# A reordered prologue, fewer pairs on VectorE, more zero matmuls and a split last block in an attention-and-convolution kernel

## The chip, the cores and the metric

The kernel runs on one core of one Trainium2 chip. The metric is the device time of one execution in microseconds (us). The span of a profiled execution, from its first to its last instruction, is about 2 us shorter than the device time (907.9 against 909.96 for the kernel before). Executions of one kernel differ in the clock granted to TensorE (0.993 to 1.000 in the runs of the kernel before), so the mean granted clock is given beside a time where it matters (1.000 is full speed).

The engines are TensorE (PE, its weight loads PEld), VectorE (DVE), ScalarE (ACT), GpSimd (POOL) and SyncE (SP). A "q" behind a name, such as SPq or ACTq, is that engine's issuing of transfers.

## The reference

Two results of the same input x (2048 rows of 640) are mixed by a gate. Cut to what matters:

```python
g = sigmoid((x * gate_w).sum(-1, keepdims=True))
# a: short convolution of k (4 taps) times v, long convolution by FFT, + kv*D, times q
# b: attention, 32 heads of 20, one shared key and value head
q = (x @ wq).reshape(B, S, 32, 20).transpose(0, 2, 1, 3)
k = x @ wk;  v = x @ wv
p = softmax(einsum("bhqd,bkd->bhqk", q, k) * 20 ** -0.5)
b = einsum("bhqk,bkd->bhqd", p, v)...reshape(B, S, 640) @ wo
return g * a + (1 - g) * b
```

The 32 heads x 2048 queries x 2048 keys need 134 million exponentials. They are computed in 2048 tiles of 128 x 512: 32 groups, each of 16 key blocks and 4 tiles.

## The kernel before

The kernel is written as a list of operations with costs and priorities. A list scheduler in the same file gives every engine its order and places the semaphores. A change of a priority, a constant or a list therefore reorders a large part of the program. ScalarE takes the tiles in units of three and two (ETA, ETB) from two sets of PSUM banks, while TensorE computes the scores of the next unit and multiplies the finished ones with the values (PV, into bank 6):

```python
def EXP(n):
    lo, w = 512 * base[n % 2], 512 * len(units[n])
    op("act", lambda e: e.activation(et(n)[:, 0:w], self.ps[:, lo:lo + w], ACT.Exp, scale=SCALE),
       [("ps", base[n % 2] + k) for k in range(len(units[n]))], [("ET", n % 4)], c_exp(w), name="exp", main=True,
       after=self.sins if n == 0 else ())
```

Some pairs of tiles are taken from ScalarE. DVE_J has one entry for each of the 32 groups, and each number in it is a key block of which VectorE exponentiates two tiles, by six instructions. The convolution, the projections and the output projection fill the gaps of TensorE.

Where a gap is left, the scheduler puts in a *zero matmul*: it adds zeros to bank 6, so it changes nothing. It is placed if, by the scheduler's own estimates, TensorE was busy for less than the share FILL of the last 2.4 us. It is not allowed between the last PV of a group and the first of the next (`can_fill`), as bank 6 is read then:

```python
if (self.filler is not None and self.main_started and self.can_fill and m is not None and gap > 0.1
        and self.busy_in(t, 2.4) < FILL):          # FILL = 0.55
    f = Op("pe", self.filler, c_mm(512), "c", "fill", 0.0)
...
self.can_fill = not op.last
...
sch.filler = lambda e: e.matmul(self.bank(6), self.T["zeros"][:, :], self.T["Tcos"][:, 0, 0:512], start=False,
                                stop=False)
```

The prologue has its own zero matmuls (filler0), under the same FILL. It brings x transposed: block 3 of 512 rows by a plain load and transposes on TensorE, blocks 0 to 2 by transposing transfers:

```python
self.dma(T["xn"][:, 12:16, :], x[:, 12:16, :], writes=[("xn", 3)], nbytes=655360, prio=-9)
for b in range(NB - 1):
    o = T["xT"][:, :, 512 * b:512 * b + 512]
    i = aps["A_q"][0][512 * b:512 * b + 512, :]
    xl = self.g.add("sp", lambda e, o=o, i=i: e.dma_start_transpose(o, i), (), [("xT", b)], 0.1, kind="d", ...)
```

After these come 20 matmuls of 41 columns for each block (k, v and gate), the query projection of block 0 (10 matmuls of 512 columns), a bound on the scores, a small transfer that puts it under the queries (qT<-cr), and the first scores.

The tail evicts the four last output blocks and stores them:

```python
for ci in range(4):
    ...
    self.dve(lambda e, ci=ci, i=i, osb=osb: e.scalar_tensor_tensor(
        ..., T["omgf"][:, i:i + 1], T["part"][:, ci, :]..., ALU.mult, ALU.add), ..., name="op2_ev")
    self.dma(self.aps["out"][0][128 * i:128 * i + 128, :], osb[:, :], reads=[("outsb", ci)],
             nbytes=163840, prio=p, name="st_out", eng="act" if ci % 2 else "sp")
```

## Time and profile before

The median of the first three runs is 908.3 us (907.63 to 909.58). The profiled run took 909.96 us, at a mean clock of 0.998.

| part of the span of 907.9 us | us | what limits it |
|---|---|---|
| to the start of the first exponential | 25.3 | transfers of x, projections, one small transfer |
| first to last exponential | 873.3 | ScalarE, busy for 870.4 |
| after the last exponential | 9.3 | evictions and stores |

The lines behind the table stand in the prediction. In them, the busy time of an engine in a stage is followed by its number of instructions, and the clock of a stage stands behind the engines.

### The profile page before, as it was taken

How to read it: one execution, taken by the hardware profiler on the slowest of the kernel's cores; microseconds unless marked ns; L12 is line 12 of the kernel's file. 1: busy time of each engine (PE TensorE's matmuls, PEld its weight loads, DVE VectorE, ACT ScalarE, POOL GpSimd, SP SyncE). 2: the span in 40 equal slices, each digit the busy share in tenths (PEclk: the TensorE clock that was granted, in tenths of full speed). 3: DMA queues.
4: the chain of work that ended last, by engine and by line, in shares of the span. 5: the costliest groups of instructions: out<-in, count | busy, mean ns of one | idle time of the engine just before them, and what ended most of it. 6: DMA issues, size and time to landing. Idle time of an engine off the chain costs nothing.

```text
span 907.9 us, 16333 instructions
## 1 busy us (share of the span) xinstructions
PE 853.1 (94%) x6950; PEld 350.7 (39%) x7013; DVE 631.9 (70%) x878; ACT 883.9 (97%) x791; POOL 380.2 (42%) x330
## 2 busy tenths in 40 slices
PE   6999999999999999999999999999999998998897
PEld 3344344443433344343333333343443332432233
DVE  5446743456766668876887778876678896787964
ACT  5999999999999999999999999999999999999995
POOL 2940056870426396154685213769125495000000
PEclk9999999999999999999999999999999999999999
DMA  7940300010000010000010200000000000301111
GB/s 162 200 134 9 65 19 20 7 37 18 20 19 14 9 41 19 19 19 13 13 37 19 56 20 13 19 8 18 20 19 14 18 4 25 93 13 35 64 35 52
DMA packets 58507, 32.69 MB, mean 36 GB/s; under 512 B 41154, under 2 KB 54466, under 8 KB 58434
## 3 DMA queue, kind: packets, MB, share of 16 engines
q1 hardware_dynamic: 56168, 31.05, 12.7%
q8 instruction: 55, 0.90, 0.4%
q10 hardware_dynamic: 2266, 0.59, 0.3%
q14 instruction: 18, 0.15, 0.1%
HBM read 18.01 MB, written 6.02 MB: 26 GB/s over the span
## 4 chain that ended last, share of the span: by engine, by line
ACT 64%; PE 29%; DMA 3%; SPq 2%; DVE 2%; issue 1%; DVEq 0%
ACT ETA L1055 39%; ACT ETB L1055 25%; PE ps L1023 8%; PE ps L1336 6%; PE ps L1097 6%; PE ps L1400 3%; PE ps L949 2%; PE ps L1270 1%; DMA kTr<-in_A_k_dram 1%; SPq L1253 1%; DMA rbc<-scr_d 1%; DMA xT<-in_A_q_dram 1%; PE ps L1434 1%; PE ps L1187 1%; SPq L722 1%
## 5 line engine op out<-in xcount | busy, mean ns | idle before, releaser
L1055 ACT ACTIVATE ETA<-ps 128x1536 bf16<-128x1536 f32 x384 | 571.3, 1488 | 3.5 <-PE ps L1097 2.2
L1055 ACT ACTIVATE ETB<-ps 128x1024 bf16<-128x1024 f32 x383 | 410.3, 1071 | 0.2 <-PE ps L1023 0.2
L1023 PE MATMUL ps<-qT,kT 21*128 21x512 bf16 x2048 | 302.5, 384 | 34.6 <-ACT ETA L1055 22.7
L1367 POOL TENSOR_TENSOR Pp<-X,K 128x512 f32<-128x512 bf16 x120 | 168.6, 1430 | 358.2 <-DVE K L1355 350.8
L1097 PE MATMUL ps<-ETA,vaug 128*32 128x512 bf16 x1150 | 196.1, 389 | 0.4 <-DVE acc L1151 0.3
L1097 PE MATMUL ps<-ETB,vaug 128*32 128x512 bf16 x766 | 188.1, 389 | 0.0
L1023 PEld LDWEIGHTS ps<-qT,kT 21*128 21x128 bf16 x2048 | 74.7, 91 | 223.2 <-ACT ETA L1055 122.9
L1085 DVE TENSOR_SCALAR dJ<-ps 128x512 uint32<-128x512 f32 x132 | 90.7, 687 | 43.8 <-PE ps L1023 43.4
L1093 DVE SCALAR_TENSOR_TENSOR ETd<-dJ,dE 128x1024 bf16<-128x1024 f32 x66 | 89.4, 1354 | 19.5 <-PE ps L1097 19.4
L1090 DVE SCALAR_TENSOR_TENSOR dE<-dJ,dE 128x1024 f32<-128x1024 uint16 x66 | 89.9, 1362 | 0.5
L1092 DVE SCALAR_TENSOR_TENSOR dJ<-dJ 128x1024 f32<-128x1024 uint16 x66 | 89.3, 1353 | 0.4
L1367 POOL TENSOR_TENSOR AB<-Pp 128x256 bf16<-128x256 f32 x80 | 77.4, 967 | 4.9
L1400 PE MATMUL ps<-AB,Tcos 128*128 128x256 bf16 x320 | 78.2, 275 | 0.8 <-DVE dJ L1085 0.6
L1097 PEld LDWEIGHTS ps<-ETA,vaug 128*32 128x32 bf16 x1150 | 47.7, 93 | 65.6 <-issue 63.0
L1400 PE MATMUL ps<-AB,Tsin 128*128 128x256 bf16 x280 | 69.3, 275 | 0.0
L1097 PEld LDWEIGHTS ps<-ETB,vaug 128*32 128x32 bf16 x766 | 45.3, 92 | 43.5 <-issue 42.9
L1367 POOL TENSOR_TENSOR Pp<-Pp 128x512 f32<-128x512 f32 x40 | 60.9, 1524 | 2.7
L1088 DVE TENSOR_SCALAR dE<-dJ 128x1024 uint32<-128x1024 uint32 x66 | 54.1, 820 | 0.5
L1336 PE MATMUL ps<-ssm_kT,Tsin 128*128 128x256 bf16 x320 | 53.7, 275 | 0.0
L1336 PE MATMUL ps<-kv,Tsin 128*128 128x256 bf16 x320 | 53.7, 275 | 0.0
L1336 PE MATMUL ps<-kv,Tcos 128*128 128x256 bf16 x320 | 52.0, 275 | 1.2 <-DVE kv L1410 0.5
L1336 PE MATMUL ps<-ssm_kT,Tcos 128*128 128x256 bf16 x320 | 51.8, 275 | 0.4 <-DVE dJ L1085 0.3
(135 smaller groups left out, 807.5 us busy)
## 6 DMA issues: line engine op xcount, KB each, us to landing
rbc<-scr_d SPq DMA_DIRECT2D x31, 256.0 KB
scr_o<-oTn SPq DMA_DIRECT2D x24, 128.0 KB, 1.8
xn<-in_A_q_dram SPq DMA_DIRECT2D x4, 640.0 KB
kv<-in_A_v_dram SPq DMA_DIRECT2D x4, 640.0 KB, 5.3
out_dram<-outsb SPq DMA_DIRECT2D x14, 160.0 KB, 1.8
oTp<-scr_o SPq DMA_DIRECT2D x12, 160.0 KB, 5.2
wog<-in_B_wo_dram SPq DMA_DIRECT2D x4, 200.0 KB
wo<-in_B_wo_dram SPq DMA_DIRECT2D x4, 200.0 KB, 3.3
```

The source lines that it names most:

```text
L949: o = self.mm(gr, lambda e, bk, gi=gi, dc=dc: e.matmul(self.bank(bk), T["wq_pad"][:, dc, 128 * gi:128 * gi + 128], T["xT"][:, dc, 512 * I: ...
L1023: return e.matmul(self.bank(bk), T["kT4"][32 * r:32 * r + 21, 128 * j:128 * j + 128], T[f"qT{G // 8 % 2}"][32 * r:32 * r + 21, G % 8, :], ...
L1055: op("act", lambda e: e.activation(et(n)[:, 0:w], self.ps[:, lo:lo + w], ACT.Exp, scale=SCALE), [("ps", base[n % 2] + k) for k in range(le ...
L1085: self.evac(gr, "dve", lambda e, bk, h=h: e.tensor_scalar(J[:, 512 * h:512 * h + 512], self.bank(bk), SCALE * LOG2E * 65536.0, EOFF * 6553 ...
L1088: V(lambda e: e.tensor_scalar(E[:, :], J[:, :], 7, 0x7F800000, ALU.logical_shift_left, ALU.bitwise_and), [kJ], ["dE"], c_fast(1024), **k)
L1090: V(lambda e: e.scalar_tensor_tensor(Ef, lo, ED, Ef, ALU.add, ALU.mult), [kJ, "dE"], ["dE"], c_ps(1024), **k)
L1092: V(lambda e: e.scalar_tensor_tensor(Jf, lo, EP, lo, ALU.add, ALU.mult), [kJ], [kJ], c_ps(1024), **k)
L1093: V(lambda e: e.scalar_tensor_tensor(T["ETd"][:, :], Jf, EQ, Ef, ALU.add, ALU.mult), [kJ, "dE"], ["ETd"], c_ps(1024), **k)
L1097: return op("pe", lambda e: e.matmul(self.bank(6)[32 * r:32 * r + 32, :], T["vaug"][:, j, :], src, start=(j == 0), stop=(j == NSC - 1), ti ...
L1336: o = self.mm(gr, lambda e, bk, lhs=lhs, rhs=rhs, comp=comp, n=n: e.matmul(self.bank(bk, 256, 256 * comp), lhs, rhs, start=(n == 0), stop= ...
L1367: f = lambda e: e.tensor_tensor(out, a, b, alu)
L1400: self.mm(gr, lambda e, bk, lhs=lhs, fc=fc, comp=comp, h=h: e.matmul(self.bank(bk, 256, 256 * h), lhs, AB[:, fc, :, comp, :], start=(fc == ...
```

## The change

It tries to make the start shorter and to relieve VectorE, and it has four parts.

1. **Prologue.** Blocks 2 and 3 of x come by plain loads and are transposed on TensorE; only blocks 0 and 1 come by transposing transfers. Priorities bring the projection, the squares and the evictions forward, and ScalarE's table load for Exp waits for the squares.
2. **Pairs.** VectorE gets 62 pairs in place of 66, in other groups.
3. **Zero matmuls.** FILL rises from 0.55 to 0.7: 281 of them in place of 149 in the long stage. The prologue has 18 in both.
4. **Tail.** Of the four last output blocks, block 1 is scaled by ScalarE and added to by GpSimd, beside VectorE.

```diff
-FILL = 0.55
+FILL = 0.7
-DVE_J = [(), (), (), (), (), (6,), (2, 9), (2, 9), (2, 9), (2, 9), (2, 9), (3, 7, 11, 13), ...]     # 66 pairs
+DVE_J = [(), (), (), (6,), (), (2,), (3, 7, 11, 13), (2, 6, 11), (2, 9), (2, 9), (2, 9), (2, 9), ...] # 62 pairs
+NX = 2
...
-        self.dma(T["xn"][:, 12:16, :], x[:, 12:16, :], writes=[("xn", 3)], nbytes=655360, prio=-9)
-        for b in range(NB - 1):
+        for b in range(NX, NB):
+            self.dma(T["xn"][:, 4 * b:4 * b + 4, :], x[:, 4 * b:4 * b + 4, :], writes=[("xn", b)], nbytes=655360,
+                     prio=-9)
+        for b in range(NX):
...
-            gr = self.group("kT", (1.16 if b == 0 else 4.0) + 0.1 * b, banks=ALLB if b == 0 else (7, 4, 5))
+            gr = self.group("kT", (1.95 if b == 0 else 4.0) + 0.1 * b, banks=ALLB if b == 0 else (7, 4, 5))
...
+        self.warm.deps.update(self.g.writer[("ksq", b)] for b in range(NB))
...
+            if ci == 1:
+                tmp = T["dE"][:, 0:D].bitcast(F32)
+                self.op("act", ... e.activation(tmp..., self.ps[...], ACT.Copy, scale=T["omgf"][:, i:i + 1]) ...)
+                self.pool(lambda e, ci=ci, osb=osb, tmp=tmp: e.tensor_tensor(osb[:, :], tmp, T["part"][:, ci, :], ALU.add), ...)
+            else:
               self.dve(... scalar_tensor_tensor as before ...)
```

Cut are the order of the gate_w load and the priorities of some evictions and squares of the prologue.

More of the change, by code (lines that the diff above doesn't have):

```diff
@@ L512 @@
 SIDE = (7, 5)
-DVE_J = [(), (), (), (), (), (6,), (2, 9), (2, 9), (2, 9), (2, 9), (2, 9), (3, 7, 11, 13), (2, 9), (6,), (3, 8, 13), (2, 9), (3, 9), (2, 9), (3, 7, 11, 13), (2, 7, 12), (2, 7), (3, 9), (2, 7), (1, 5, 9), (2, 7, 12), (3, 8, 13), (4, 11), (2, 6, 11), (2, 6, 11), (1, 4, 8, 12), (2, 9), (1, 5, 9)]
+DVE_J = [(), (), (), (6,), (), (2,), (3, 7, 11, 13), (2, 6, 11), (2, 9), (2, 9), (2, 9), (2, 9), (3, 8, 13), (2, 9), (2, 9), (2, 9), (2, 9), (2, 9), (4, 11), (2, 9), (3, 9), (2, 9), (2,), (3, 8, 13), (2, 9), (2, 7), (2, 9), (2, 7, 12), (3, 8, 13), (3, 9), (3, 8, 13), (2, 7, 12)]
 MAC_ALT = ()
+NX = 2
 SCALE = float(DH) ** -0.5
@@ L713, in loads @@
         self.dma(T["gw5"][:, :], aps["gate_w"].rearrange("(dc p) -> dc p", p=128), writes=["gw5"], nbytes=2000,
-                 eng="act", prio=-98.65)
+                 eng="act", prio=-98.9, lat=6.2)
         self.dma(T["wqst"][:, :, 0:160], wq[:, :, 0:160], writes=[("wqst", 0)], nbytes=204800, eng="act", prio=-98.6)
@@ L723, in loads @@
                             nbytes=655360, prio=-8 + b, lat=1.6)
-            xl.iss = 3.3
+            xl.iss = 4.8 if b == 0 else 3.3
         self.xl = [xl]
@@ L799, in tables @@
                             ["warm"], 1.5, prio=-1500.0, after=list(sins)))
+        self.warm = sins[-1]
         self.sins = sins
@@ L858, in xT @@
         T = self.T
-        b = NB - 1
-        for d0, nd in ((0, 2), (2, 2), (4, 1)):
-            gr = self.group("xT", 1.0, banks=(0, 1, 2, 3, 4, 5, 7))
+        for b, d0, nd in [(b, d0, nd) for b in range(NX, NB) for d0, nd in ((0, 2), (2, 2), (4, 1))]:
+            gr = self.group("xT", 1.0 + 0.01 * b, banks=(0, 1, 2, 3, 4, 5, 7))
             for dc in range(d0, d0 + nd):
@@ L870, in xT @@
                 "p (d t) -> p d t", d=nd), True)
-            self.evac(gr, "dve", None, (), [("xT", b)], 0.45, alts=al)
+            self.evac(gr, "dve", None, (), [("xT", b)], 0.45, alts=al, prio=-2000.0)
     def load_x(self):
@@ L875, in load_x @@
         x = self.aps["A_q"][0].rearrange("(i p) d -> p i d", p=128)
-        for b in range(NB - 1):
+        for b in range(NX):
             self.dma(T["xn"][:, 4 * b:4 * b + 4, :], x[:, 4 * b:4 * b + 4, :], writes=[("xn", b)], nbytes=655360,
@@ L908, in kproj @@
                         self.bank(bk, 41, 44 * ci), T["xT"][:, dc, 128 * tc:128 * tc + 128], T["wkv"][:, dc, 0:41],
-                        start=(dc == 0), stop=(dc == NDC - 1)), [("xT", b), "wk", "wv", "wg"], 0.05)
+                        start=(dc == 0), stop=(dc == NDC - 1)), [("xT", b), "wk", "wv", "wg"], 0.03)
             def view(bk, lo, n=20):
@@ L913, in kproj @@
             self.evac(gr, "act", lambda e, bk, b=b, view=view: e.activation(
-                T["ksq"][:, 4 * b:4 * b + 4, :], view(bk, 0), ACT.Square), (), [("ksq", b)], c_act(80))
+                T["ksq"][:, 4 * b:4 * b + 4, :], view(bk, 0), ACT.Square), (), [("ksq", b)], c_act(80), prio=-4500.0)
             self.evac(gr, "dve", lambda e, bk, b=b, view=view: e.tensor_copy(T["vaug"][:, 4 * b:4 * b + 4, 0:20],
@@ L945, in qproj @@
         par = I % 2
+        first = I == 0 and gs[0] == 0
         for gl, gi in enumerate(gs):
@@ L957, in qproj @@
             self.evac(gr, "dve", None, (), [("qT", par, gi)], 0.7,
-                      alts=self.copy_alts(qt[:, gi, :], lambda bk: self.bank(bk)))
+                      alts=self.copy_alts(qt[:, gi, :], lambda bk: self.bank(bk)), prio=-2500.0 if first else None)
             self.dve(lambda e, gi=gi, gl=gl: e.tensor_tensor(T[f"sq{gl}"][:, :], qt[:, gi, :], qt[:, gi, :],
                                                              ALU.mult),
-                     [("qT", par, gi)], [("sq", gl)], c_fast(512), prio=prio - 500, port=True, name="sq")
-        gr = self.group("q2", prio - 500, banks=banks)
+                     [("qT", par, gi)], [("sq", gl)], c_fast(512), prio=-5500.0 if first else prio - 500, port=True, name="sq")
+        gr = self.group("q2", -5500.0 if first else prio - 500, banks=banks)
         ind = T[f"IndG{ng}"]
@@ L969, in qproj @@
         ci, cr = T["ci"], T["cr"]
-        pr = -5000.0 if I == 0 and gs[0] == 0 else prio - 500
+        pr = -5000.0 if first else prio - 500
         self.evac(gr, "dve", lambda e, bk: e.tensor_scalar(
@@ L1232, in tail @@
                 mm(ci, half, 7)
-            self.dve(lambda e, ci=ci, i=i, osb=osb: e.scalar_tensor_tensor(
+            if ci == 1:
+                tmp = T["dE"][:, 0:D].bitcast(F32)
+                self.op("act", lambda e, ci=ci, i=i, tmp=tmp: e.activation(
+                    tmp.rearrange("p (h n) -> p h n", h=2),
+                    self.ps[:, 1024 * ci:1024 * ci + 1024].rearrange("p (h n) -> p h n", h=2)[:, :, 0:HD],
+                    ACT.Copy, scale=T["omgf"][:, i:i + 1]), ["omgf", ("ps", 2 * ci), ("ps", 2 * ci + 1)], ["dE"],
+                    c_act(D), prio=p, name="op2_ev")
+                self.pool(lambda e, ci=ci, osb=osb, tmp=tmp: e.tensor_tensor(osb[:, :], tmp, T["part"][:, ci, :], ALU.add),
+                          ["dE", ("part", ci)], [("outsb", ci)], c_pool(D), prio=p, port=True, name="op2_ev")
+            else:
+              self.dve(lambda e, ci=ci, i=i, osb=osb: e.scalar_tensor_tensor(
                 osb[:, :].rearrange("p (h n) -> p h n", h=2),
```

## The prediction

> **What bounds the kernel now.** I read the views in this order: the busy times by stage, the costliest groups, the timeline of the first 26 us and of the last 10 us, and the start times of all 767 exponentials from the timeline of ScalarE. The stages first (columns: busy us and instruction count of each engine, granted clock, DMA share, GB/s):
>
> ```profile
> core 0: us, PE busy (x) PEld busy (x) DVE busy (x) ACT busy (x) POOL busy (x), PEclk, DMA share, GB/s
> 0.00:25.30 25.30, 18.40 (x155) 8.72 (x157) 13.79 (x55) 13.55 (x23) 6.11 (x19) 0.93 0.66 146
> 25.30:898.60 873.30, 830.22 (x6764) 339.33 (x6824) 611.97 (x815) 870.36 (x768) 374.11 (x312) 1.00 0.12 32
> 898.60:907.90 9.30, 4.45 (x34) 2.68 (x32) 6.09 (x9) 0.01 (x1) 0.00 (x0) 0.95 0.26 91
> ```
>
> The run is a prologue of 25.3 us (until the first exponential starts), a stage of 873.3 us in which ScalarE is busy for 870.4, and a tail of 9.3 us after the last exponential. In the long stage ScalarE is the bound: VectorE has 261 us free, GpSimd 499. The work is nearly all in two rows of the costliest groups:
>
> ```profile
> L1055 ACT ACTIVATE ETA<-ps 128x1536 bf16<-128x1536 f32 x384 | 571.3, 1488 | 3.5 <-PE ps L1097 2.2
> L1055 ACT ACTIVATE ETB<-ps 128x1024 bf16<-128x1024 f32 x383 | 410.3, 1071 | 0.2 <-PE ps L1023 0.2
> ```
>
> The idle time before them is 3.7 us in all, so waits hardly matter. The two durations overlap: from start to start, by the timeline, the median is 1.33 us for a 1536-wide one and 0.91 for a 1024-wide one, 2.24 for a pair of five 512-column tiles. The mean pair is 872.65 us / 383 = 2.279. The 14 us above 383 x 2.24 are about 60 intervals lengthened by 0.13 to 0.9 us (eleven of them by over 0.3, together some 5 us) and jitter.
>
> The prologue is a chain of transfers, projections and one small transfer:
>
> ```profile
> 1.25 11.25 SPq L722 DMA_TRANSPOSE xT<-in_A_q_dram  x3
> ...
> 12.16 0.68 PE L907 MATMUL ps<-wkv,xT 128*128 128x41 bf16 x20 [1.55 <-DMA xT<-in_A_q_dram]
> ...
> 13.05 3.63 PE L949 MATMUL ps<-xT,wq_pad 128*128 128x512 bf16 x9 [0.22 <-issue]
> ...
> 22.74 0.73 SPq L565 DMA_DIRECT2D qT<-cr  x1
> ...
> 25.30 1.45 ACT L1055 ACTIVATE ETA<-ps 128x1536 bf16<-128x1536 f32 x1 [0.78 <-PE ps L1023]
> ```
>
> TensorE waits until 12.1 for the second transposed block of x although the query projection (L949) needs only the first; then those ten 512-column matmuls run slowly. Their starts in the timeline are 0.43 us apart instead of 0.22, and the stretches with the clock (PE busy, clock among the columns above) say why:
>
> ```profile
> 12.60:16.30 3.70, 3.48 (x18) 1.39 (x15) 2.13 (x10) 1.53 (x4) 0.00 (x0) 0.54 0.63 127
> 16.30:18.00 1.70, 1.70 (x23) 0.99 (x22) 1.28 (x6) 1.28 (x3) 0.00 (x0) 1.00 0.96 325
> ```
>
> Nine intervals x 0.21 = 1.9 us are lost to half clock. The tail ends with four VectorE evictions and a last store:
>
> ```profile
> 902.27 3.26 DVE L1233 SCALAR_TENSOR_TENSOR outsb<-ps,omgf,part 128x640 bf16<-128x640 f32 x4 [0.54 <-PE ps L1211]
> ...
> 905.56 0.36 ACTq L565 DMA_DIRECT2D out_dram<-outsb  x1
> ```
>
> [...]first matmuls 0.43 us apart until about 6 us, half clock again for about 3.6 us from 12.65, after 1.6 us idle. [...]Here transposes move 230 to 290 GB/s, the plain load of x some 350 (3.0 to 4.5 us). [...]
>
> **The change, part by part.**
>
> *Fewer pairs on VectorE.* The two lists hold 66 and 62 pairs. A pair is two 512-column tiles whose exponential VectorE computes in about 6.3 us (2 x 0.69 + 0.82 + 1.36 + 1.35 + 1.35). So 8 tiles move to ScalarE: 1916 become 1924. On the path: 8/5 x 2.279 = **+3.65 us**; nothing hides it, as ScalarE is full. VectorE gets 25 us back, which are worth nothing in themselves. They can only shorten intervals in which TensorE waited for a late VectorE pair; of the 5 us in long intervals I grant 0.5. The groups with four pairs go from three to one, and that one (group 6) comes early.
>
> *More zero matmuls.* The order of instructions shows 281 instead of 149 in the long stage, and 18 as before in the prologue. 132 x 0.216 = 28 us of TensorE time, in gaps. In the long stage the clock is already 1.00, so nothing can be won; intervals with zero matmuls in them are no longer than the others (mean excess 0.02 to 0.04 us against 0.045 in those without), so I count 0.
>
> *Prologue.* Blocks 2 and 3 of x now come by plain loads ahead of two transposing DMAs, and TensorE transposes both (40 matmuls, 6 evictions, 3 on each of two engines). The same bytes move, but the block that the projection needs comes third. One more plain load of 655 KB at 350 GB/s is 1.8 us: the first transposed block, which released TensorE at about 9.7, should land near 11.3. After it stand 60 matmuls of 41 columns (2.0 us at the measured 0.66 per 20) and the ten of the projection (2.2 us at full clock): they end at 15.5, against 16.7 before. Then, by the order: the last 20 of 41 columns (0.6), five key matmuls (1.1), four zero matmuls (0.9), the small ones (0.7): 18.8. Two VectorE steps of 0.67 and 0.47 with four of 0.14 between: 20.5. The small transfer took 1.86 from issue to landing: 22.4. Scores and start: 0.7. The first exponential would start at **23.1** at full clock. The table load and the squares no longer stand in the way (before, squares waited behind the table load until 20.0). At half clock the 60 small matmuls take about 1.6 us more and a part of the projection 0.5: 24.6 to 25.2. The idle time before the block lands is about 1.4 us (before 1.6)[...]: I give full clock 4 chances in 10. Mean: 0.4 x 23.1 + 0.6 x 24.9 = 24.2, so **-1.1 us**.
>
> *Tail.* VectorE does three evictions of 0.82 us instead of four and ends at about 904.7 instead of 905.5. The other block: ScalarE starts at about 902.55, takes 0.79 (a 512-column one with a pointer takes 0.69, plus 128 x 0.83 ns), and GpSimd adds. Its nearest row:
>
> ```profile
> L1367 POOL TENSOR_TENSOR Pp<-Pp 128x512 f32<-128x512 f32 x40 | 60.9, 1524 | 2.7
> ```
>
> For 640 columns that is an estimated 1.9 us: 905.3. And the order shows that ScalarE's queue issues this block's store ahead of the last block's, which so waits for GpSimd: issues at about 905.4 and 905.8, against 905.56 before. **0.0 to +0.3 us, say +0.1**: the 0.8 us saved are taken back.
>
> Sum: 3.65 - 0.5 - 1.1 + 0.1 = +2.1 us, 910.4. I lower it to **909.5**, since a new list of pairs may remove more of the long intervals than I can see.
>
> **Rivals.** First: the prologue gains much more, since a projection that is not held for the second block and stays at full clock saves 1.9 us at once; with 3 us gained and long intervals halved (-2.5) the time would be 906. For it: the idle 1.6 us and the half clock are plainly visible; against: the needed block now stands third in the queue. Second: the prologue gains nothing or loses, as [...]the transfers are slower than I think (kT-like transposes beside plain loads took 4.5 to 5.0 us to issue, against 3.0 alone): 912 to 913. Third: TensorE becomes the bound by its zero matmuls. It shows busy for 830 of 873 us, but that is modelled; 2.28 us per pair hold 5 scores and 5 value matmuls that overlap in groups. If each of the 132 delayed ScalarE by 0.03 us it would be 4 us; the intervals above speak against it.
>
> **Range and chances.** Prologue -3 to +0.5, stage +1 to +5.5, tail +-0.4, run to run +-1: 906 to 912.5. Two per cent are 18 us, which is out of reach both ways: within 2% 0.98.
>
> **What would show it.** The first exponential at 23 to 25.2 us (a later one: the block landed later); the clock between 11 and 17 us, 1.00 or about 0.5; the stage from first to last exponential 874 to 877.5 us, with the median pair still at 2.24; in the tail a GpSimd addition of 1.5 to 2 us and the last two stores issued after it by ScalarE. I would be wrong if the long stage grew by less than 2 us though 8 tiles came to it (then late pairs cost more than I saw), if the pair interval itself moved, or if the clock fell in the long stage.

## The result, and the profile after

The changed kernel took 909.79 us (median of 4 runs, 909.53 to 910.33); the kernel before took 908.87 in the median of its 4. The ratio is 1.0012, with a 95% interval from 0.9995 to 1.003. A ratio here is the mean time of one kernel's fast runs over the mean time of the other's fast runs of the same rounds, so it is not quite the ratio of the medians quoted. Executions over 1.5% slower than the fastest of the same kernel are left out of the means. The results are correct.

The stages of the changed kernel (columns as in the prediction):

```profile
0.00:22.45 22.45, 18.56 (x175) 9.70 (x175) 15.05 (x57) 14.72 (x25) 5.83 (x19) 1.00 0.69 164
22.45:898.76 876.31, 867.35 (x6958) 351.34 (x6958) 592.24 (x790) 874.36 (x772) 367.48 (x312) 1.00 0.12 32
898.76:908.50 9.74, 4.31 (x32) 2.74 (x32) 4.84 (x7) 0.80 (x2) 1.53 (x1) 0.99 0.19 68
```

The prologue is 2.85 us shorter than in the profile of before, the long stage 3.00 longer and the tail 0.45 longer: +0.6 us for the span. ScalarE is busy for 874.36 us of its stage where it was 870.36. The stage changed by the work given to ScalarE, and the rest of that time still holds next to no waits, as the costliest groups show (count, busy us, mean ns, idle before them):

```profile
L1061 ACT ACTIVATE ETA<-ps 128x1536 bf16<-128x1536 f32 x385 | 570.0, 1480 | 1.7 <-PE ps L1029 0.4
L1061 ACT ACTIVATE ETB<-ps 128x1024 bf16<-128x1024 f32 x385 | 407.7, 1059 | 0.3 <-PE ps L1029 0.3
...
L1499 PE MATMUL ps<-Tcos,zeros 128*128 128x512 bf16 x281 | 87.1, 384 | 0.0
```

The starts of the exponentials are 1.33 and 0.90 us apart in the median, as before. What the intervals hold above those medians is 16.5 us in all, against 17.0 before.

The timeline of the prologue after (start, length, engine, line, what was written from what, count, idle time before and what ended it), for the lines that the prediction shows of before:

```profile
1.78 9.27 SPq L726 DMA_TRANSPOSE xT<-in_A_q_dram  x2
...
11.23 1.17 PE L911 MATMUL ps<-wkv,xT 128*128 128x41 bf16 x40
...
13.11 2.32 PE L955 MATMUL ps<-xT,wq_pad 128*128 128x512 bf16 x10
...
19.95 0.73 SPq L567 DMA_DIRECT2D qT<-cr  x1
...
22.45 1.45 ACT L1061 ACTIVATE ETA<-ps 128x1536 bf16<-128x1536 f32 x1
```

And the stretch from 11 to 17 us, with the clock (1.00) behind the engines:

```profile
11.00:17.00 6.00, 5.81 (x98) 3.75 (x97) 5.36 (x21) 5.30 (x12) 0.63 (x1) 1.00 0.78 203
```

The ten matmuls of the projection now take 2.3 us in one row, where nine of them took 3.63. The clock stays at full speed after the transfer has landed, and the small transfer is issued 2.8 us earlier.

The timeline of the tail after:

```profile
902.35 2.47 DVE L1250 SCALAR_TENSOR_TENSOR outsb<-ps,omgf,part 128x640 bf16<-128x640 f32 x3 [0.61 <-PE ps L1217]
902.62 0.79 ACT L1242 ACTIVATE dE<-ps,omgf 128x640 f32<-128x640 f32 x1 [3.86 <-PE ps L1217]
...
903.49 1.53 POOL L1247 TENSOR_TENSOR outsb<-dE,part 128x640 bf16<-128x640 f32 x1 [150.67 <-ACT dE L1242]
...
905.05 0.86 ACTq L567 DMA_DIRECT2D out_dram<-outsb  x2
```

VectorE is done at 904.82 and GpSimd at 905.02. ScalarE's queue issues the stores of blocks 1 and 3 one behind the other after that, until 905.91. From there to the end of the span are 2.6 us; before, the last store was issued by 905.92 and 2.0 us followed.

### The profile page after: what moved, and what is told of

Same layout as the page of the kernel before. It is cut to its first block, busy times and chain, and to the rows that moved or that the text cites. A ratio compares the mean times of both kernels' runs of the same rounds, so it can differ in the third digit from the quotient of the medians.

```text
span 908.5 us, 16687 instructions
## 1 busy us (share of the span) xinstructions
PE 890.2 (98%) x7165; PEld 363.8 (40%) x7165; DVE 612.1 (67%) x854; ACT 889.9 (98%) x797; POOL 374.8 (41%) x331
## 4 chain that ended last, share of the span: by engine, by line
ACT 52%; PE 38%; issue 5%; DMA 1%; DVE 1%; POOL 0%; SPq 0%; POOLq 0%
ACT ETA L1061 32%; ACT ETB L1061 20%; PE ps L1029 11%; PE ps L1353 8%; PE ps L1103 8%; PE ps L1417 5%; PE ps L1499 2%; PE ps L955 2%; PE ps L1287 1%; DMA kTr<-in_A_k_dram 1%; PE ps L1451 1%; PE ps L1503 1%; POOL Pp L1384 0%; PE ps L971 0%; SPq L1270 0%
## 5 line engine op out<-in xcount | busy, mean ns | idle before, releaser
L1384 POOL TENSOR_TENSOR Pp<-X,K 128x512 f32<-128x512 bf16 x120 | 166.5, 1413 | 346.4 <-DVE K L1372 345.5
L1091 DVE TENSOR_SCALAR dJ<-ps 128x512 uint32<-128x512 f32 x124 | 85.1, 686 | 36.3 <-PE ps L1029 35.3
L1099 DVE SCALAR_TENSOR_TENSOR ETd<-dJ,dE 128x1024 bf16<-128x1024 f32 x62 | 84.1, 1356 | 22.1 <-PE ps L1103 21.6
L1096 DVE SCALAR_TENSOR_TENSOR dE<-dJ,dE 128x1024 f32<-128x1024 uint16 x62 | 86.9, 1401 | 0.7
L1499 PE MATMUL ps<-Tcos,zeros 128*128 128x512 bf16 x281 | 87.1, 384 | 0.0
L1098 DVE SCALAR_TENSOR_TENSOR dJ<-dJ 128x1024 f32<-128x1024 uint16 x62 | 83.2, 1342 | 0.2
```

The lines of the kernel that those rows point to most:

```text
L1091: self.evac(gr, "dve", lambda e, bk, h=h: e.tensor_scalar(J[:, 512 * h:512 * h + 512], self.bank(bk), SCALE * LOG2E * 65536.0, EOFF * 6553 ...
L1096: V(lambda e: e.scalar_tensor_tensor(Ef, lo, ED, Ef, ALU.add, ALU.mult), [kJ, "dE"], ["dE"], c_ps(1024), **k)
L1098: V(lambda e: e.scalar_tensor_tensor(Jf, lo, EP, lo, ALU.add, ALU.mult), [kJ], [kJ], c_ps(1024), **k)
L1099: V(lambda e: e.scalar_tensor_tensor(T["ETd"][:, :], Jf, EQ, Ef, ALU.add, ALU.mult), [kJ, "dE"], ["ETd"], c_ps(1024), **k)
L1384: f = lambda e: e.tensor_tensor(out, a, b, alu)
```

## The experiments

My theory was the prediction's sum: a prologue that gains, eight more tiles on ScalarE that cost some 3 us, a tail that takes its gain back by the order of stores in one queue, zero matmuls that do nothing. Its rivals were that the zero matmuls delay ScalarE, that they carry the clock, and that the shorter prologue came from the clock alone. All runs gave correct results. All that follow are on one chip except w1_hole_filled, whose runs of the kernel before are its own. Each had five rounds. Ratios are against the kernel before. By the line of 2% all are rated "same" except x1_prologue (unclear) and y3_nozero (slower), so what follows on differences of a few us rests on the intervals and on the traces.

### The prologue alone: x1_prologue

The changed kernel with the other three parts undone. Its scheduler leaves out two of the prologue's 18 zero matmuls, so even the prologue is not quite the same:

```diff
-FILL = 0.7
+FILL = 0.55
-DVE_J = [... 62 pairs ...]
+DVE_J = [... the 66 pairs of before ...]
-            if ci == 1:
+            if ci == 99:
```

> The changed kernel with 66 pairs, old zero-matmul rule and old tail: of the four parts only the prologue stays. My theory (the parts add up: prologue -2.9 us as the first exponential came at 22.45 instead of 25.30 in the two profiles, pairs +3.0, tail +0.4, zero matmuls 0) expects 2 to 3.2 us less than before, about 906.0. Its own scheduler puts the key projection before the query projection here and leaves out two zero matmuls, so the first exponential may come at 22.5 to 23.5. Rival (the prologue's gain is an accident of one profile[...]): within 1 us of before.

Measured: 930.11 us (919.05 to 934.25), a ratio of 1.0207 (1.0158 to 1.0256), rated unclear. The first exponential starts at 22.74, near the 22.45 of the full change, but the long stage took 886.67. TensorE in stretches, with the clock (columns: length, PE busy and count, clock, DMA share, GB/s):

```profile
575.00:580.00 5.00, 3.94 (x36) 1.00 0.00 0
580.00:585.00 5.00, 4.79 (x25) 0.64 0.03 3
585.00:610.00 25.00, 25.00 (x128) 0.50 0.05 16
610.00:615.00 5.00, 5.00 (x28) 0.50 0.01 3
615.00:620.00 5.00, 4.92 (x40) 0.95 0.00 0
```

For some 34 us TensorE ran at half clock in the middle of the long stage, and the profile shows it busy for all of that time (25.00 of 25.00 us, by modelled ends). The timeline shows what came just before:

```profile
580.21 0.39 PE L1029 MATMUL ps<-qT,kT 21*128 21x512 bf16 x3 [0.95 <-ACT ETA L1061]
```

It had stood idle for 0.95 us, and 1.2 us after the end of that hole, at 581.4, its matmuls became slow. The clocks of the six runs were 0.957 to 0.983, and the times follow them: 919.05 us at 0.983, 932.1 at 0.961 (a slow run of 934.25 at 0.957 is left aside). So this run does not isolate the prologue: a change in the program's start reordered the long stage, and its clock fell. It raised the question of what the zero matmuls are for.

### The list of pairs alone: x2_62pairs

The kernel before with the 62 pairs in place of the 66, nothing else (151 zero matmuls in the long stage).

```diff
-DVE_J = [... 66 pairs ...]
+DVE_J = [... 62 pairs ...]
```

> The kernel before with only the new list of 62 pairs. Theory: 8 more tiles on ScalarE, stage from first to last exponential longer by 3.0 us (as between the two profiles) to 3.65, so 3 to 3.7 us slower, about 912. Rival (fewer pairs pay by fewer long intervals): less than 2 us slower.

Measured: 913.96 us (911.87 to 918.65), ratio 1.0063 (1.0033 to 1.0093), clocks 0.987 to 0.998. In its profile too the clock fell, for some 7 us:

```profile
480.00:488.60 8.60, 7.59 (x60) 1.00 0.23 46
488.60:495.00 6.40, 6.40 (x29) 0.50 0.00 0
```

Its two runs at a clock of 0.998 took 911.87 and 911.96. The kernel before took 907.88 to 909.47 in its four runs at that clock, 908.6 in the mean. The list alone costs about 3.3 us where the clock is alike, near the predicted 3.15, and further time where it falls.

### The tail alone: x3_tail

The kernel before with the split block alone.

```diff
+            if ci == 1:
+                (ScalarE scales into dE, GpSimd adds, as in the change)
```

> The kernel before with only the split tail. Theory: the eviction saved on VectorE (0.8 us) is taken back because ScalarE's queue issues two stores one after the other behind the GpSimd addition: 0 to +0.5 us. Rival (the longer tail of the changed kernel's profile, 9.74 against 9.29, was chance and the split pays): 0.4 to 0.8 us faster.

Measured: 908.11 us (907.82 to 910.14), ratio 0.9996 (0.9974 to 1.0017). The time can't tell 0.1 us from 0.4. The tail of the profile is 9.64 us; in the three profiles with the old tail it is 9.24 to 9.30. The engines behave as in the changed kernel (ScalarE 0.79 us, GpSimd 1.53, both late stores on ScalarE's queue).

The profile serves a second purpose. It has the old prologue, with the idle time before the second block, and the clock nevertheless held:

```profile
12.44 0.68 PE L907 MATMUL ps<-wkv,xT 128*128 128x41 bf16 x20 [1.73 <-DMA xT<-in_A_q_dram]
12.96 1.24 PE L949 MATMUL ps<-xT,wq_pad 128*128 128x512 bf16 x5
```

Its first exponential starts at 24.00. Half clock in the old prologue thus varies from profile to profile: of its four, two have it (25.30 and 25.40, with a mean clock of 0.93 up to there) and two do not (24.00 and 24.07, with 1.00).

### The change with as few zero matmuls as before: x4_fill55

```diff
-FILL = 0.7
+FILL = 0.55      # long stage: 149 zero matmuls; the prologue keeps 0.7
```

> The changed kernel with the old number of zero matmuls in the long stage (149 instead of 281), all else as changed, the prologue too. Theory: the clock is 1.00 in the stage either way, so within 0.5 us of the changed kernel (909.8). Rival A (the added zero matmuls delay scores): 1 to 3 us faster. Rival B (they keep the clock or shorten the long intervals): over 1 us slower, with a granted clock under 1.00 somewhere in the stage.

Measured: 911.31 us (910.32 to 913.39), ratio 1.0028 (1.0006 to 1.005). Four runs had a clock of 1.000 (mean 910.9) and two of 0.995 and 0.996 (913.39, 912.79).

```profile
23.25:900.37 877.12, 844.61 (x6826) 341.63 (x6826) 595.46 (x790) 874.30 (x772) 372.24 (x312) 1.00 0.12 32
```

TensorE is busy for 23 us less than with 281, yet the stage is 0.8 us longer, not shorter. So the added zero matmuls did not delay ScalarE (stages of 876.31 and 877.12 us).

### The changed kernel again: y1_after

No edit.

> The changed kernel itself, on the chip of the next three and with more rounds, as their reference. Expected: 909.5 to 910.5, within 0.3% of before, granted clock 0.998 to 1.000 in every run (it was so in its four runs).

Measured: 909.98 us (908.95 to 912.34), ratio 1.0017 (0.9992 to 1.0042). First exponential 22.12, stage 876.15, tail 9.63: the three stages repeat within 0.4 us. Against it, x4_fill55 is slower by 1.2 us in the mean of all runs and by 1.35 in those at a clock of 1.000. It was run at another time. So the sign is not firm.

### The old pairs with many zero matmuls: y2_66f65

With the 66 pairs of before and FILL = 0.7 the scheduler finds no end, as its last matmuls find no room, so 0.65 was used (220 zero matmuls).

```diff
-FILL = 0.7
+FILL = 0.65      # the prologue keeps 0.7
-DVE_J = [... 62 pairs ...]
+DVE_J = [... the 66 pairs of before ...]
```

> The changed kernel with the old list of 66 pairs, and zero matmuls between the two kernels' numbers (220 in the long stage; with 281 its scheduler finds no end). The prologue's instructions are those of the changed kernel. The first set left one question: the prologue with 66 pairs and 143 zero matmuls ran 919 to 934 us, as the clock stood at 0.50 from 581 to 615 us. Theory (TensorE was too idle there and zero matmuls are what prevents it): clock 0.998 or more, and 3 to 3.7 us faster than the changed kernel, about 906.5. Rival (66 pairs with the new prologue make a hole that zero matmuls do not fill, or pairs late on VectorE stall the stage): a clock under 0.99 and over 912 us.

Measured: 913.33 us (912.83 to 931.03, the longest a slow run at a clock of 0.970), ratio of fast runs 1.005 (1.0027 to 1.0073). The stage took 881.87 us in the profile, with half clock from about 552 to 569 us, after two holes of 0.60 and 0.42 us within 1.4 us. 220 zero matmuls did not keep the clock here.

### No zero matmuls in the long stage: y3_nozero

```diff
-FILL = 0.7
+FILL = 0.0       # the prologue keeps 0.7
```

> The changed kernel without any zero matmul in the long stage (0 instead of 281); the prologue's stay. My prediction counted them as worth 0. Theory as it stands after the first set (they keep TensorE busy enough that the clock does not fall): stretches of clock 0.50 in the stage, mean clock 0.95 to 0.99 and 5 to 25 us slower than the changed kernel, differing from run to run by several us. Rival (as predicted, worth nothing): within 1 us of it.

Measured: 1005.71 us (1002.78 to 1016.73), ratio 1.108 (1.1035 to 1.1125), clocks 0.834 to 0.855. The bulk of the long stage, and ScalarE's largest group:

```profile
24.00:960.00 936.00, 890.02 (x6495) 337.96 (x6493) 573.83 (x772) 854.79 (x744) 363.86 (x311) 0.85 0.11 29
```

```profile
L1062 ACT ACTIVATE ETA<-ps 128x1536 bf16<-128x1536 f32 x385 | 566.5, 1471 | 77.7 <-PE ps L1030 46.7 <-PE ps L1104 29.4
```

ScalarE's own instructions are as long as before, but it waits 77.7 us for TensorE before its wide ones, where it waited 1.7. TensorE has less to do, takes more time for it (890 us busy), and becomes the bound. Up to 900 us it stood idle for 0.5 us or more some 40 times (28 us in all; 4 times and 3.1 us in the changed kernel), and its score matmuls (L1030) took 436 ns in the mean, against 384 in the changed kernel. The zero matmuls are what keeps this kernel at full clock: 0.85 for the stage without them, 1.00 with 281.

### The split block's store on the other queue: y4_storesp

```diff
-nbytes=163840, prio=p, name="st_out", eng="act" if ci % 2 else "sp")
+nbytes=163840, prio=p, name="st_out", eng="act" if ci == 3 else "sp")
```

> The changed kernel with the split block's store issued by SyncE (after its other two) instead of by ScalarE, so that the last block's store no longer waits for the GpSimd addition. Theory (the queue order takes the saving back): the last block's store is issued at about 904.9 instead of 905.5 and the other at 905.1, and the run is 0.2 to 0.6 us faster than the changed kernel. Rival (the end is set by the addition and the landing of its store alone): within 0.1 us.

Measured: 909.12 us (908.51 to 911.33, and one slow run of 929.42 at a clock of 0.973), ratio of fast runs 1.0005 (0.9979 to 1.0031). The tail is 8.93 us:

```profile
902.28 2.12 SPq L567 DMA_DIRECT2D out_dram<-outsb  x3
...
903.86 0.37 ACTq L567 DMA_DIRECT2D out_dram<-outsb  x1
```

ScalarE issues block 3 at once, and SyncE issues block 1 after GpSimd. GpSimd's addition ends at 904.04, and the last issue at 904.40 in place of 905.91, while this run's last exponential ended 1.0 us earlier than the changed kernel's; 2.3 us follow. With the same two engines doing the same work, the tail is 0.7 us shorter than in y1_after, so what took the gain back was the order of two stores in one queue (three later profiles with this order have tails of 8.86 to 8.93). In the time it is 1.1 us in the mean of fast runs, inside their scatter.

### The old prologue with the rest of the change: z1_oldpro

The kernel before with the new pairs, FILL of 0.7 in the long stage (282 zero matmuls; 0.55 in the prologue) and the new tail.

```diff
-FILL = 0.55
+FILL = 0.7       # the prologue keeps 0.55
-DVE_J = [... 66 pairs ...]
+DVE_J = [... 62 pairs ...]
+            if ci == 1: (as in the change)
```

> The changed kernel with the old prologue: 62 pairs, the new tail and 282 zero matmuls in the long stage, so that the clock holds in the stage, unlike in the first set's attempt to show the prologue alone. Theory: the first exponential at 24.0 us, or at 25.3 where the clock halves at 12.6 us (seen in one of three profiles of the old prologue), against 21.7 to 23.25 in six profiles of the new: 1.7 to 2.5 us slower than the changed kernel, about 912. Rival (the new prologue takes part of its gain back in the first stretch of the stage): under 1 us slower.

Measured: 915.76 us (912.42 to 924.32), ratio 1.0091 (1.0054 to 1.0127), clocks 0.987 to 1.000. Two falls of the clock stand in the profile, one in the prologue and one in the stage, the latter behind an idle stretch:

```profile
12.00:16.00 4.00, 3.59 (x28) 0.57 0.72 143
...
745.60:755.00 9.40, 9.40 (x57) 0.64 0.51 121
```

```profile
745.29 0.39 PE L1024 MATMUL ps<-qT,kT 21*128 21x512 bf16 x3 [0.95 <-ACT ETA L1056]
```

Its two runs at a clock of 1.000 took 912.42 and 912.52; those of y1_after took 908.95 to 910.25, 909.5 in the mean. That is 2.9 us for the new prologue, if nothing else differed. The stage was ordered anew, so this is a rough estimate; the start times of the first exponential measure the prologue better. The rival's mechanism, a gain that is partly taken back in the first stretch of the stage, is in the traces; "Why the prediction was right or wrong" has the numbers.

### Other lists of pairs: z2_64pairs and z3_66pairs

Both start from y4_storesp. The first gives two groups one more pair each (64) and raises FILL to 0.8 (300 zero matmuls). The second adds two more pairs (66 again, but not those of before) at 0.7 (251 zero matmuls).

```diff
 z2: FILL = 0.8 (prologue 0.7); DVE_J[5] = (2, 9); DVE_J[22] = (2, 9)
 z3: FILL = 0.7;                DVE_J[5] = (2, 9); DVE_J[22] = (2, 9); DVE_J[9] = (2, 7, 12); DVE_J[14] = (2, 7, 12)
```

> Attempt at a version that beats both: the changed kernel with the split block's store on SyncE, two pairs more on VectorE (64: one more in groups 5 and 22, which had one each), and 300 zero matmuls. Theory (a pair is worth 0.9 us as long as the clock holds): 1.6 us faster than the same with 62 pairs (909.1), about 907.5, clock 0.998 or more. Rival (any move of the pairs opens holes in TensorE's work): clock under 0.997 and over 910.

> The same with four pairs more (66, in groups 5, 9, 14 and 22) and 251 zero matmuls, as its scheduler finds no end with more. Theory: 3.3 us faster than with 62 pairs, about 905.8, if the clock holds at 251 zero matmuls. Rival (66 pairs leave too little room for zero matmuls, as in the runs with the old list of 66): a stretch of clock 0.50, over 910.

Measured for z2_64pairs: 912.68 us (911.56 to 923.5), ratio 1.0067 (1.0033 to 1.0101), clocks 0.983 to 1.000. The most zero matmuls so far, and the clock fell again, after a hole of 0.95 us:

```profile
770.35 0.39 PE L1030 MATMUL ps<-qT,kT 21*128 21x512 bf16 x3 [0.95 <-ACT ETA L1062]
```

Measured for z3_66pairs: 907.17 us (906.59 to 907.85), ratio 0.9983 (0.997 to 0.9996), a clock of 1.000 in all five runs. It has the shortest time of all versions, ahead of both kernels by a little. Its long stage:

```profile
23.00:896.79 873.79, 864.84 (x6928) 350.07 (x6928) 614.13 (x814) 870.70 (x769) 378.97 (x312) 1.00 0.12 31
```

With 66 pairs the stage is back to within 0.5 us of before, with the short prologue (23.0 us) and the short tail (8.9) beside it. It holds the clock with fewer zero matmuls than two versions that lost it. So their number does not decide it.

### The holes at the groups' ends closed: w1_hole_filled

The holes of 0.95 us stand where a zero matmul is not allowed, at the end of a group. Here z2_64pairs may put one there into a side bank (7 or 5) that is free.

```diff
+            if (self.filler is not None and self.main_started and not self.can_fill and m is not None and gap > 0.1
+                    and ... and self.busy_in(t, 2.4) < FILL):
+                for b in (7, 5):
+                    if bank b is free: zero matmul into it, start=True, stop=True
```

> The 64-pair version (z2, 912.7 us, clock 0.983 to 1.000) with one rule more: zero matmuls may also stand where a head group's sums are being read out, into a free bank, which the old rule forbids. The order of instructions shows 308 instead of 300 zero matmuls, and the two score units that stood side by side at 770 us, with 0.95 us of idle TensorE between them, no longer do. In all five profiles with a fallen clock in the stage the fall came 0 to 2 us after such a hole (two score units with nothing between, or a wait of that length). Theory (the hole, not the number of zero matmuls, lets the clock fall): no hole of 0.8 us late in the stage, clock 0.998 or more in most runs, about 908. Rival (the clock falls for another reason): clock 0.997 or less and 911 to 913 again.

Measured on another chip: 909.02 us (908.3 to 909.94), ratio 0.999 (0.9977 to 1.0004), clocks 0.999 or 1.000 in all five runs, and 1.00 for the whole stage in the profile. The place that corresponds to the hole, in its timeline:

```profile
767.88 0.39 PE L1038 MATMUL ps<-qT,kT 21*128 21x512 bf16 x2
768.20 1.04 PE L1510 MATMUL ps<-Tcos,zeros 128*128 128x512 bf16 x4
769.17 0.39 PE L1038 MATMUL ps<-qT,kT 21*128 21x512 bf16 x3
```

Four zero matmuls fill it, with only eight more in all than z2_64pairs. Idle times of 0.5 us or more sum to 1.4 us in this stage. The ratio went from 1.0067 to 0.999. The stage took 876.01 us, though by its tiles (four fewer than in the changed kernel's 876.31 us, at 0.45 us each from the median intervals) I estimate some 1.5 us less; where that went is open. That it ran on another chip is a rival; the kernel before was no steadier there, with clocks of 0.996 to 1.000.

### What the runs say together on the clock

| run | zero matmuls in the stage | fall of the clock in the profiled stage | clocks of the fast runs |
|---|---|---|---|
| x1_prologue | 143 | yes | 0.961 to 0.983 |
| x2_62pairs | 151 | yes | 0.987 to 0.998 |
| y2_66f65 | 220 | yes | 0.989 to 0.994 |
| z1_oldpro | 282 | yes | 0.987 to 1.000 |
| z2_64pairs | 300 | yes | 0.983 to 1.000 |
| x4_fill55 | 149 | no | 0.995 to 1.000 |
| y1_after | 281 | no | 0.998 to 1.000 |
| z3_66pairs | 251 | no | 1.000 |
| w1_hole_filled | 308 | no | 0.999 to 1.000 |

In the five profiles with one, the first slow matmul comes 0.3 to 1.7 us after a hole: one of 0.95 us in three of them, several of 0.4 to 0.6 us in x2_62pairs and y2_66f65. The half clock then lasted 3.4 us in z2_64pairs, some 7 us in x2_62pairs and z1_oldpro, 17 us in y2_66f65 and some 34 us in x1_prologue. The theories of x1_prologue, y2_66f65, z1_oldpro and z2_64pairs, which added up parts at full clock, missed by this. A hole is not enough, though. The changed kernel has the same one, without a fall behind it:

```profile
741.35 0.39 PE L1029 MATMUL ps<-qT,kT 21*128 21x512 bf16 x3 [0.95 <-ACT ETA L1061]
```

That the holes matter is shown by y3_nozero (28 us of holes of 0.5 us or more, a clock of 0.85) and, less firmly, by w1_hole_filled (1.4 us, a clock of 1.00). Why the clock fell after one hole of 0.95 us and not after another was not shown: no run moves a hole and leaves the rest as it was.

## Why the prediction was right or wrong

The predicted 909.5 us stands beside 909.79 measured (909.98 when repeated), and "within 2%" held. The terms of the sum:

- **Fewer pairs (+3.65 and -0.5, so +3.15): right in size, partly by luck.** The stage grew by 3.00 us between the two profiles; the three profiles of the changed stage (876.31, 876.15, 876.06) stand 3.3 above the two of the old one (873.31, 872.37) in the mean. The median intervals did not move, as predicted; at them, eight tiles are 3.6 us. The excess above the medians fell by 0.5, as granted, but as the sum of two larger parts. The intervals longer by over 0.3 us went from 11 with 5.0 us together to 5 with 2.0, while the many small excesses grew by 2.6. Some of that growth belongs to the prologue: in the first 15 us of the stage the excess is 0.1 to 0.3 us in the four profiles of the old prologue and 0.95 to 1.3 in nine of the new (y3_nozero has 3.5). One part of it is seen: in the changed kernel TensorE waits 0.94 us at 33.9 for a transfer of the convolution (kTr), and the exponential after it starts 0.39 us late.
- **Prologue (-1.1): the mechanism was right, the chance of the clock was mis-sized.** The steps came out as predicted, each a little early: the first block at 11.23 (11.3 predicted), the projection's end at 15.43 (15.5), VectorE's chain at 19.92 (20.5), the first exponential at 22.45 (23.1). The step that failed is "I give full clock 4 chances in 10", an estimate of mine, and with it the idle time of 1.4 us that it rests on: TensorE never stood idle for more than 0.32 us between 7.5 and 17 us, as transposes, zero and small matmuls filled the wait for the block. Nine profiles of the new prologue, mean 22.50 us, show full clock every time, 1.00 in each stretch of 2 us from 7 to 21 us (x1_prologue, ordered otherwise, does so too). The baseline was mis-sized as well: 25.30 was a draw with half clock, and the old prologue's four profiles have a mean of 24.69. So the gain is 2.2 us in the means, and 1.5 where both have full clock. It was partly the clock and partly the order. About 1.0 of it is taken back in the first 15 us of the stage, so the net gain of some 1.2 us stands near the predicted 1.1 by luck. The first rival, that the prologue gains some 3 us, was right for the two profiles that were compared, but not for the mean. Its halved long intervals came, but the small ones made up for them, and the 906 us did not come.
- **Zero matmuls (0): the number held for 149 against 281, the reason did not reach far enough.** I wrote that the clock is already 1.00, "so nothing can be won". It was at 1.00 with 149 in place; without any, the changed kernel loses 96 us to y1_after. (That the kernel before would lose as much is not shown.) Single parts of the change, with other orders of the same work, lose the clock for 7 to 34 us. The rival that zero matmuls delay ScalarE falls by x4_fill55: fewer of them made nothing faster.
- **Tail (+0.1, at most +0.3): right in the reason, a little small.** GpSimd took 1.53 us, not the 1.9 estimated in proportion to 1524 ns for 512 columns (its additions of 256 columns took 967 ns in the kernel before, those of 512 took 1430 to 1524). The issue of the last store ended 7.15 us after the last exponential, against 7.32 before; but the end of the span followed 2.6 us after it, against 2.0. Over the six profiles with the split block and its old queue order (y3_nozero left out) the tail is 9.36 to 9.79 us, 9.64 in the mean, against 9.24 to 9.30 in the three without: about +0.4. That the queue's order takes the gain back was predicted, and y4_storesp shows it (8.93 us). Why two stores issued back to back end later after the last issue is open.
- **The lowering from 910.4 to 909.5: right in size, for another reason.** I lowered for long intervals that the new list might remove. They shrank, but the stage as a whole grew no less than the sum had it; the larger gain of the prologue stands in their place. With the terms as measured, -2.2 + 3.3 + 0.4 = +1.5 us, which agrees with the ratios of 1.0012 and 1.0017 (+1.1 and +1.5 us).
- **One reading was loose.** The 830 us for which the prediction shows TensorE busy are too few, as that trace lacks 38 of the 149 zero matmuls.

So the change trades some 2 us of prologue for 3 us of exponentials. It comes out even, with a more stable clock than most partial versions had.

## What to carry to other kernels

Cut the span at the stages' ends and ask what each part of a change is worth in its own stage; here eight tiles moved onto the bounding engine came with a stage 3.0 us longer, though the helper engine was busy in it for 592.24 us in place of 611.97. When a profile shows a full clock, ask what keeps it there before counting the idle work beside it as worthless (here 1.00 with the zero matmuls and 0.85 without), and after each reordering look at the clock of the stages and at the holes ahead of a fall. Here a store waited for the producer of the one ahead of it in its queue, and the tail was 0.7 us shorter once it did not (y4_storesp), so put a store that becomes ready late where nothing follows it.
